# Batch 1's k and q loaded two pairs to a transfer, and w_out's copies made for two pieces at a time

## The chip, the cores and the metric

The kernel runs on one core of a Trainium2 chip. The metric is the time of one execution on the device in microseconds (us), the median of several runs. Beside them one execution was recorded by the hardware profiler; its rows are what is called the profile, or the trace, below. The engines are TensorE (PE for its matmuls, PEld for its weight loads), VectorE (DVE), ScalarE (ACT), GpSimd (POOL) and SyncE (SP), which here does nothing but issue transfers (DMAs). Sixteen DMA engines carry the transfers of the core.

## What is computed

An attention block with a threshold, and a feed-forward block behind it. All arrays are float32 except the two weights, which arrive as float64: their product with a float64 scalar makes them so.

```python
# q, k, v: (8 batches, 8 heads, 576, 64); tau = 0.02
scores = scale * np.matmul(q, k.transpose(0, 1, 3, 2))       # scale = 1/8
thresh = np.max(scores, axis=-1, keepdims=True) - tau
scores = np.where(scores >= thresh, scores, -1000000000.0)
scores = scores - np.max(scores, axis=-1, keepdims=True)
attn = np.exp(scores)
attn = attn / (np.sum(attn, axis=-1, keepdims=True) + 1e-09)
x = np.matmul(attn, v)                                       # -> (4608, 512), heads side by side
h = x @ w_in                                                 # w_in 512 x 1024
e = np.exp(h - np.max(h, axis=-1, keepdims=True))
solu = h * (e / (np.sum(e, axis=-1, keepdims=True) + 1e-09))
ln = (solu - mean(solu)) / np.sqrt(var(solu) + 1e-06) * g_ln
out = ln @ w_out                                             # w_out 1024 x 512
```

## The kernel before

**Tiling.** A head's 576 rows of 64 numbers are read as 64 rows of 576 (NK = 9 tokens to a row), and two heads, a pair, lie in the 128 partitions: head 0 in rows 0 to 63, head 1 in rows 64 to 127 (ROWS). There are 4 pairs in a batch (NP) and 32 in all. Scores need k and q turned, so that the 64 numbers of a head lie in the partitions (kT, qT).

**Rounds.** The program is one long loop over 144 rounds (rnd), 18 to a batch (PER). A round issues, in an order that is written out by hand and that each engine follows: the scores of one slot (line 399) after the turns that are due in front of them; the row maxima on VectorE (line 420); the threshold and the exponentials on ScalarE (lines 435 and 444); the sums and the normalising of the slot before on GpSimd (lines 451 to 454); a step of the feed-forward block, which is a half of x @ w_in (ff_h, line 570) or a half of ln @ w_out (ff_o, line 675); and the product of the weights with v (line 507) for a unit of two slots, LAG_PV = 3 rounds after its second slot (4 at slot 11). Then blocks turns the weights of the slot before on VectorE (line 466) and, every second round, sends them to their rows (wT, lines 475, 477 and 482). ff_swap moves rows of the feed-forward block in the same way (V, line 652).

**k and q.** Pairs of batch 0 are loaded whole in front of the loop (load_pair, line 133). Pairs of batch 1 are loaded by load_four, four heads at a time: for e = 0 and 1 a tile raw of 128 partitions receives head e of pair i in rows 0 to 63 and head e of pair i + 1 in rows 64 to 127 (j = 0 and 1, lines 141 and 142). The call stands in rounds 10 (k of pairs 4 and 5), 11 (q), 15 (k of pairs 6 and 7) and 16 (q). The turns that read them are matmuls with the identity (turn_beside, line 344), from round 14 and round 19 on; each needs both tiles of its k or q. Pairs of later batches come by load_natural (line 168) and are turned on VectorE and by copies (line 188).

**The weights.** w_in and w_out come in 16 pieces (piece): 0 to 7 are w_in's, 8 to 15 are w_out's. VectorE, ScalarE and GpSimd make float32 out of each (weight_e, weight_m, weight_b, weight_c). Of w_out there are two versions in the tile w2, of 16 entries: entry 2c is piece c as it is, and entry 2c + 1 is the same with the two halves of the partitions exchanged. weight_d makes the second with two transfers of 64 rows (line 312; both sides show up as `w` in the trace). It is called in the round after the piece is ready, so for c = 0 to 7 in rounds 8 to 15. ff_o reads entry m ^ r; its first half reads entries 0 to 7, its second half 8 to 15. It does not start before w2_done, which is set in round 15.

**Order on the queue.** All of these transfers are issued by SyncE, in program order. Within a round the order is: wT's copies, V's, the loads of raw weights, weight_d, and then what load_at holds for the round (load_four, load_v, load_natural). Each transfer can wait for what its source or its place is waiting for, and all behind it wait too. The completion of a transfer is told by one of eight semaphores, used in turn.

Of the kernel before, what the change touches and what calls it, by code (L numbers as in the profile page):

```python
# [20 lines left out]
def kernel(  # L21
# [27 lines left out]
    nc = tc.nc  # L49
# [10 lines left out]
    ROWS = (slice(0, 64), slice(64, P))  # L60
# [10 lines left out]
    w2 = const.tile([P, 2 * NC, DM], F32, name="w2")  # L71
# [63 lines left out]
    def load_four(i, nm):  # L135
        heads_of = rows_of[nm][P * i : P * i + 2 * P].rearrange("(j e p) n -> e j p n", j=2, e=2)
        for e in range(2):
            tag = "ends" if nm == "q" and i > NP else nm
            raw = loads.tile([P, NK * D], F32, tag=tag, bufs=BUFS[tag], name=nm)
            whole_rows[i, nm, e] = raw.rearrange("p (m d) -> p m d", m=NK)  # L140
            for j in range(2):
                nc.sync.dma_start(out=raw[ROWS[j]], in_=heads_of[e, j])

    def load_v(b, hf, parts):
        d = halves.setdefault((b, hf), {})
# [161 lines left out]

    def weight_d(x):
        c = x - 2 * NP
        if c >= 0:  # L310
            for r in range(2):
                nc.sync.dma_start(out=w2[ROWS[r], 2 * c + 1], in_=w2[ROWS[1 - r], 2 * c])

# [423 lines left out]
    for i, at, nm in ((NP, 10, "k"), (NP, 11, "q"), (NP + 2, 15, "k"), (NP + 2, 16, "q")):  # L739
        load_at.setdefault(at, []).append(lambda i=i, nm=nm: load_four(i, nm))  # L740
# [33 lines left out]
    with tc.manual_schedule():  # L774
# [45 lines left out]
        while True:  # L820
# [157 lines left out]
            if rnd - 1 in pieces:  # L978
                weight_d(pieces[rnd - 1])
                w2_done = pieces[rnd - 1] == NW - 1  # L980
# [36 lines left out]
```

## Time and profile before

| | |
|---|---|
| median of 3 runs | 858.18 us (855.24 to 861.62) |
| the profiled execution: its time, its span | 855.96 us, 854.2 us |
| mean granted TensorE clock | 0.987 |
| TensorE matmuls busy | 819.7 us, 96% of the span |
| VectorE, ScalarE, GpSimd busy | 680.4 us (80%), 572.3 us (67%), 499.1 us (58%) |
| DMA packets, bytes moved | 75442, 168.54 MB, mean 197 GB/s |
| line 142, k: 8 transfers of 144 KB | issued from 69.0 to 98.4 us, median 3.4 us to landing |
| line 142, q: 8 transfers of 144 KB | issued from 74.3 to 105.0 us, median 4.4 us to landing |
| line 312: 16 transfers of 128 KB | issued from 56.9 to 95.8 us, median 4.6 us to landing |

Busy is the time in which an engine had an instruction at work; matmuls are pipelined, so a busy TensorE need not be at its peak. The chain that ended last is followed back from the last instruction: at each step to what released it, or to the instruction before it on its engine. Landing is counted from the issue on the queue. A window is a stretch of the span, in us from its start.

### The profile page before, as it was taken

Reading aid. Unit: us, or ns where it says so; the run is one execution under the profiler, and the core shown is the slowest. Engines: PE = TensorE matmul, PEld = TensorE weight load, DVE = VectorE, ACT = ScalarE, POOL = GpSimd, SP = SyncE. Lnnn points to the kernel's source line nnn. Section 1 sums busy time; section 2 is a strip of 40 time slices with the busy share of each in tenths; the row PEclk is TensorE's granted clock in tenths of the full one; section 3 lists DMA queues with packets and bytes.
Section 4 is the critical chain, followed back from the end, with each engine's and each line's share of the span. In section 5 each row is a group of like instructions: output and inputs, shape, how many; then the busy total and the mean of one; then the engine's idle time right before and its main releaser. Section 6 shows DMA issues by size and latency. Waiting matters only on the chain.

```text
span 854.2 us, 36120 instructions
## 1 busy us (share of the span) xinstructions
PE 819.7 (96%) x15363; PEld 613.4 (72%) x15363; DVE 680.4 (80%) x1241; ACT 572.3 (67%) x1127; POOL 499.1 (58%) x945
## 2 busy tenths in 40 slices
PE   6679889999999999999999999999999999999997
PEld 5456666667677787777688877777777777777655
DVE  6999868889788888888788878888888888787361
ACT  6888857877666666666676667766667777775121
POOL 3888637666556656565566666565666655555120
PEclk8889999999999999999999999999999999999999
DMA  9989897898889788887889787888888887655212
GB/s 339 265 236 231 208 206 185 227 250 208 225 208 227 194 191 205 219 214 181 216 212 220 194 177 200 212 212 212 200 207 228 202 195 188 154 136 140 67 39 63
DMA packets 75442, 168.54 MB, mean 197 GB/s; under 512 B 11274, under 2 KB 32786, under 8 KB 75282
## 3 DMA queue, kind: packets, MB, share of 16 engines
q1 hardware_dynamic: 74994, 165.82, 77.3%
q8 instruction: 120, 1.97, 1.0%
q10 hardware_dynamic: 288, 0.43, 0.2%
q14 instruction: 40, 0.33, 0.1%
HBM read 46.14 MB, written 9.44 MB: 65 GB/s over the span
## 4 chain that ended last, share of the span: by engine, by line
PE 80%; DVE 7%; DMA 6%; ACT 3%; issue 2%; POOL 1%; SPq 1%; DVEq 0%; ACTq 0%
PE o_ps L675 27%; PE h_ps L570 21%; PE s_ps L399 15%; PE pv L507 14%; DMA wT<-T 4%; PE h_ps L560 3%; DVE T L466 2%; DVE w L420 2%; ACT w L435 1%; ACT w L444 1%; DVE w L290 1%; DMA V<-u 1%; POOL w L454 0%; PE tp L336 0%; SPq L482 0%
## 5 line engine op out<-in xcount | busy, mean ns | idle before, releaser
L435 ACT ACTIVATE w<-s_ps,nth 128x576 f32<-128x576 f32 x280 | 196.9, 738 | 110.5 <-DVE nth L420 92.0
L675 PE MATMUL o_ps<-w,uT 64*64 64x256 f32 x4608 | 268.4, 376 | 1.3 <-DVE uT L662 0.6
L675 PEld LDWEIGHTS o_ps<-w,uT 64*64 64x64 f32 x4608 | 221.0, 133 | 55.2 <-ACT xh L537 12.0
L420 DVE CUSTOM_DVE_ANT_0 w<-s_ps,tau_t 128x576 f32<-128x576 f32 x280 | 200.1, 751 | 73.7 <-PE s_ps L399 46.3
L454 POOL TENSOR_SCALAR w<-w,sm 128x576 f32<-128x576 f32 x288 | 221.3, 780 | 14.3
L466 DVE STREAM_TRANSPOSE T<-w 128x576 f32<-128x576 f32 x288 | 207.7, 756 | 24.4 <-POOL w L454 23.7
L570 PE MATMUL h_ps<-w,xh 64*64 64x512 f32 x1856 | 220.4, 590 | 0.0
L444 ACT ACTIVATE w<-w,ntau 128x576 f32<-128x576 f32 x288 | 219.5, 766 | 0.0
L507 PEld LDWEIGHTS pv<-wT,v 64*64 64x64 f32 x5760 | 170.4, 135 | 40.7 <-issue 22.9
L399 PE MATMUL s_ps<-kT,qT 64*64 64x64 f32 (+1 forms) x2048 | 173.5, 415 | 16.6 <-ACT w L435 12.5
L507 PE MATMUL pv<-wT,v 64*64 64x128 f32 (+1 forms) x5760 | 173.1, 263 | 7.2 <-DMA wT<-T 5.0
L570 PEld LDWEIGHTS h_ps<-w,xh 64*64 64x64 f32 x1856 | 114.5, 133 | 81.4 <-issue 52.1
L451 POOL TENSOR_SCALAR sm<-sm 128x2 f32<-128x2 f32 x144 | 36.2, 252 | 194.5 <-ACT w L444 191.1
L452 POOL TENSOR_TENSOR sm<-sm,mone 128x2 f32<-128x2 f32 x144 | 108.2, 751 | 12.0
L399 PEld LDWEIGHTS s_ps<-kT,qT 64*64 64x64 f32 x2048 | 70.5, 137 | 25.4 <-ACT w L435 18.0
L537 ACT COPY xh<-pv 128x256 f32<-128x256 f32 x64 | 25.4, 397 | 72.5 <-PE pv L507 72.4
L636 ACT ACTIVATE V<-u,nb,rs 128x1024 f32<-128x1024 f32 x36 | 44.7, 1241 | 41.3 <-POOL nb L626 34.8
L662 DVE STREAM_TRANSPOSE uT<-V 128x1024 f32<-128x1024 f32 x36 | 44.3, 1231 | 21.4 <-DMA V<-u 20.7
L444 ACT ACTIVATION_READ_ACCUMULATOR w<-w,ntau 128x1 f32 x288 | 55.3, 192 | 0.0
L600 DVE TENSOR_TENSOR u<-h_ps,u 128x1024 f32<-128x1024 f32 x36 | 42.8, 1189 | 9.9 <-ACT u L594 9.9
L641 DVE TENSOR_SCALAR u<-u,rs,nb 128x1024 f32<-128x1024 f32 x36 | 34.9, 969 | 17.5 <-ACT V L636 17.4
L594 ACT ACTIVATE u<-h_ps,hm 128x1024 f32<-128x1024 f32 x36 | 40.2, 1117 | 9.9 <-DMA V<-u 5.6
(81 smaller groups left out, 563.7 us busy)
## 6 DMA issues: line engine op xcount, KB each, us to landing
wT<-T SPq DMA_DIRECT2D x160, 288.0 KB, 6.7
wT<-T SPq DMA_DIRECT2D x64, 576.0 KB, 5.5
v<-in_v_dram SPq DMA_DIRECT2D x16, 576.0 KB, 5.7
V<-u SPq DMA_DIRECT2D x144, 64.0 KB, 3.4
out_dram<-ob SPq DMA_DIRECT2D x71, 128.0 KB, 2.6
q<-in_q_dram SPq DMA_DIRECT2D x28, 288.0 KB, 6.0
k<-in_k_dram SPq DMA_DIRECT2D x27, 288.0 KB, 6.5
qT<-flip SPq DMA_DIRECT2D x48, 144.0 KB, 3.5
```

Source lines behind the costliest of these rows:

```text
L399: nc.tensor.matmul(out=ps[h][ROWS[y], ks], lhsT=lhsT, rhs=d["kT"][ROWS[h], ks], start=True, stop=True,)
L420: nc.vector.tensor_tensor_reduce(out=w, in0=ps[:, 0:S], in1=(zero if loose else tau_t).to_broadcast([P, S]), scale=1.0, scalar=BIG, op0=AL ...
L435: nc.scalar.activation(out=d["w"][x], in_=d["w"][x] if d["loose"] else d["ps"][x][:, 0:S], func=AF.Prelu, bias=d["nth"][x], scale=-1.0, al ...
L444: nc.scalar.activation(out=w, in_=w, func=AF.Exp, bias=ntau, scale=1.0, accum_out=sm[:, x : x + 1])
L452: nc.gpsimd.tensor_tensor(out=sm, in0=sm, in1=mone, op=ALU.pow)
L454: nc.gpsimd.tensor_scalar(out=w, in0=w, scalar1=sm[:, x : x + 1], scalar2=1.0, op0=ALU.mult, op1=ALU.mult)
L466: nc.vector.transpose(out=T[:, :, r, h, :], in_=w)
L507: nc.tensor.matmul(out=to, lhsT=d["v"][ROWS[u], (h0 + h - u) % 4, m,], rhs=rhs, start=m == 0, stop=m == NK - 1,)
L570: mm = nc.tensor.matmul(out=h[ROWS[y], f], lhsT=x[ROWS[r], c, ROWS[y]], rhs=w1_parts[ROWS[r], c, part ^ r], start=part == 0 and c == 0, st ...
L636: nc.scalar.activation(out=V, in_=u, func=AF.Identity, bias=nb, scale=rs)
L662: nc.vector.transpose(out=uT, in_=d["V"].rearrange("p y (m x) -> p m y x", x=32))
L675: nc.tensor.matmul(out=d["o"][ROWS[z], 512 * (r ^ other) : 512 * (r ^ other) + 256], lhsT=d["uT"][ROWS[r], m].rearrange("p y x -> p (y x)" ...
```

## The change

load_four makes one transfer out of the two of a tile: the destination is all 128 partitions of raw, and the source is heads_of[e], whose dimensions are j (2 blocks, 128 rows of the array apart), p (64 rows that follow each other) and n (576 numbers). load_four is called four times, so 16 transfers of 144 KB become 8 of 288 KB.

weight_d does nothing for an even c (and for pieces of w_in, as before). For an odd c it copies pieces c - 1 and c together, once for each half of the partitions: 64 rows, two entries, 512 numbers. So 16 transfers of 128 KB become 8 of 256 KB, and the copies for c = 0, 2, 4 and 6 are made one round later than before.

```diff
@@ load_four @@
             whole_rows[i, nm, e] = raw.rearrange("p (m d) -> p m d", m=NK)
-            for j in range(2):
-                nc.sync.dma_start(out=raw[ROWS[j]], in_=heads_of[e, j])
+            nc.sync.dma_start(out=raw, in_=heads_of[e])
@@ weight_d @@
         c = x - 2 * NP
-        if c >= 0:
+        if c > 0 and c % 2:
+            pair_of = w2.rearrange("p (c two) n -> p two c n", two=2)[:, :, c - 1 : c + 1]
             for r in range(2):
-                nc.sync.dma_start(out=w2[ROWS[r], 2 * c + 1], in_=w2[ROWS[1 - r], 2 * c])
+                nc.sync.dma_start(out=pair_of[ROWS[r], 1], in_=pair_of[ROWS[1 - r], 0])
```

## The prediction

> **What bounds the kernel now.** I read the page first, then the stretches of rounds 10 to 20, then that stretch of each queue. One core, no second die to compare.
>
> ```profile
> span 854.2 us, 36120 instructions
> PE 819.7 (96%) x15363; PEld 613.4 (72%) x15363; DVE 680.4 (80%) x1241; ACT 572.3 (67%) x1127; POOL 499.1 (58%) x945
> ...
> q1 hardware_dynamic: 74994, 165.82, 77.3%
> ```
>
> TensorE is busy 96% of the span, and the chain that ended last is 80% TensorE. So a stall of TensorE is not made good later; a saving elsewhere is worth only what TensorE waits for. The edited lines run between about 57 and 106 us, so I read the table by stretches there (columns: stretch, its length, busy us of each engine with counts, granted clock, DMA share, GB/s):
>
> ```profile
> 0.00:20.00 20.00, 13.00 (x210) 9.53 (x212) 11.70 (x28) 12.09 (x23) 7.06 (x21) 0.91 0.92 340
> 20.00:45.00 25.00, 17.96 (x309) 12.65 (x309) 24.18 (x52) 21.36 (x42) 20.92 (x26) 0.77 1.02 277
> 69.00:85.00 16.00, 15.76 (x270) 11.14 (x262) 15.96 (x33) 13.93 (x28) 14.05 (x21) 1.00 0.96 235
> 97.00:111.00 14.00, 13.09 (x305) 11.38 (x304) 12.08 (x25) 9.37 (x19) 9.63 (x19) 1.00 0.89 236
> ```
>
> From 69 to 85 us TensorE and VectorE are both full and the DMA engines are 96% taken: no engine has room there, nor have the transfers. The chain of waits in order of time says what ends last (start, length, what):
>
> ```profile
> 86.69 0.61 SPq L477
> 87.29 0.04 issue
> 87.34 6.85 DMA wT<-T
> 94.19 0.04 issue
> 94.23 2.03 PE pv L507 x65
> ...
> 108.19 9.76 DMA wT<-T
> 117.96 4.37 DMA V<-u
> ```
>
> The copies wT (lines 475 to 482) and V (line 652) take 4 to 10 us to land because transfers are queued ahead of them, and twice in these rounds the chain goes through them. They have no slack worth the name. All of them leave from SyncE's queue, the one that carries the edited transfers; its timeline shows the order:
>
> ```profile
> 66.97 1.99 SPq L312 DMA_DIRECT2D w<-w  x2
> 69.01 2.52 SPq L142 DMA_DIRECT2D k<-in_k_dram  x4
> 71.64 1.02 SPq L248 DMA_DIRECT2D raw<-in_moe_w_out_dram  x1
> 73.18 1.12 SPq L312 DMA_DIRECT2D w<-w  x2
> 74.35 2.52 SPq L142 DMA_DIRECT2D q<-in_q_dram  x4
> 76.97 0.60 SPq L475 DMA_DIRECT2D wT<-T  x1
> ...
> 96.48 2.52 SPq L142 DMA_DIRECT2D k<-in_k_dram  x4
> 102.24 3.40 SPq L142 DMA_DIRECT2D q<-in_q_dram  x4
> ```
>
> And TensorE's timeline shows when they are needed: the first turn of k (line 344) at 78.6, of q at 85.0, the first product on the wT copy issued at 76.97 at 86.8 us:
>
> ```profile
> 78.61 1.45 PE L344 MATMUL s_ps<-ident,k 64*64 64x64 f32 x50
> 86.83 2.66 PE L507 MATMUL pv<-wT,v 64*64 64x128 f32 x72
> 105.88 1.48 PE L344 MATMUL s_ps<-ident,k 64*64 64x64 f32 x50
> ```
>
> **The copies of w_out (weight_d).** Sixteen transfers become eight of twice the size: the same bytes in the same 2048 B rows, 64 rows ahead as before. The copies of pieces 0, 2, 4 and 6 move one round later. That costs nothing as long as line 675 is later still. Its first half reads pieces 0 to 3 and starts at 97.97; the second, from 102.42, reads pieces 4 to 7, whose last copies are issued at 95.25 and take 4.7 us by the median of such copies here: 2.5 us of cover. SyncE saves little, for the issue of a transfer grows with its rows (0.6 us for 64 rows of k, 1.06 for the 128 of line 168). One thing moves: two copies (1.99 us at 66.97) no longer stand ahead of k in round 10, so k is issued near 67.0. Sum: zero, with a gain of at most 2 us.
>
> **The loads (load_four).** Four transfers of 64 rows become two of 128 rows; rows and bytes are the same. What changes is the shape of the source: its leading dimension was 64 (rows that follow each other) and becomes 2 (two blocks of 64 rows, 128 rows apart). Every transfer over 4 KB on the page has at least 32 rows in front. The trace has no row for a leading dimension of 2, so I bound it by two ends. At the near end the transfer is spread over all 16 engines like lines 133 and 142. At the far end its rows are dealt out by the leading dimension, and two engines carry it. The view of the DMA issues is a hint, no proof: it gives a landing time for all groups but these two, the only ones with fewer than 32 rows (1 and 8):
>
> ```profile
> tau_row<-in_tau_dram SPq DMA_DIRECT2D x1, 0.0 KB
> g_rows<-in_moe_g_ln_dram SPq DMA_DIRECT2D x1, 4.0 KB
> ```
>
> So transfers with few rows in front complete differently, and a leading dimension of 2 is nearer to these two rows than to 64. I take two engines. [...]
>
> Cost of a packet: in the first 20 us, nearly all loads from DRAM, 340 GB/s at a share of 0.92 over 16 engines is 23.1 GB/s for a busy engine, 0.100 us for the 2304 B of one row. From 69 to 85 us it is 235/(16 x 0.96) = 15.3 GB/s, 0.151 us. I take 0.100, since two engines with the rest waiting meet little contention, and keep 0.151 for the range. A transfer then holds two engines for 64 x 0.100 = 6.4 us, the two of one load_four for 12.8, where 16 engines spent 1.6. From issue to landing a 64-row load takes at least 2.8 us, 0.4 of it packets; I put 1.2 of the rest behind the last packet.
>
> *First pair of loads.* On the two engines the wT copies issued at 63.3 to 66.9 are done at about 69.5. Then k runs to 82.3 and lands at 83.5; needed at 78.6: TensorE 4.9 late. Behind it raw (8 packets an engine, 1.4 us) and two w copies (1.4): 85.1. q: 12.8 more, lands at 99.1, needed at 85.0: 14.1 late. The wT copies issued from 76.97 (16 packets of 4608 B, 3.2 to 4.8 us, take 4) land at 103.1, needed at 86.8: **16.3 late**. These are lags against one timetable, so the largest counts, not their sum. Then the backlog is gone.
>
> *Second pair* (rounds 15 and 16). Everything there is needed 16.3 later, but SyncE's queue is late too: it issues in order, and a transfer waits for one issued eight before it (the queue's waits below: a wT copy waits for a weight load that it does not read).
>
> ```profile
> SPq L652 <- DMA wT<-T: 1.8, 2, 1.0
> SPq L477 <- DMA raw<-in_moe_w_out_dram: 1.1, 1, 1.1
> ```
>
> So the third wT copy of round 14 waits for q (99.1), V and the w copies follow, and k goes out near 108.5 instead of 96.5. It lands at 108.5 + 1.2 + 12.8 + 1.2 = 123.7 against 105.9 + 16.3 = 122.2: 1.5 late. The next wT copies: 127.7 against 124.5, 3.2 late. q behind them: 126.5 + 12.8 + 1.2 = 140.5 against 110.9 + 16.3 = 127.2: **13.3 late**. The later wT copies (146.1 against 137.1) and V (148.6 against 138.6) follow, less late.
>
> *Clock.* The granted clock was 0.77 from 20 to 45 us, where TensorE was busy 72%, and 1.00 from 69 us. With stalls of some 30 us in the next 70, matmuls between them could run at less: 15 us of them at 0.77 would be 4.5 more. I take 2. [...]
>
> **Sum.** 16.3 + 13.3 + 2 = 31.6 us. On the profiled execution (855.96, its span 854.2 and 1.8 around it) this gives 887.6; that run lies 2.2 under the median of three (855.24 to 861.62), so I name 858.2 + 31.6 = **890 us**.
>
> **The rivals.** *Sixteen engines, a queue relieved.* If the source's leading dimension does not matter, k and q land as now, and SyncE saves two thirds of a microsecond here and there. Place: the wT copies in rounds 12 to 18. TensorE waits 3.3 us for them from 60 to 130 us; saving part of it gives 856, all of it and the 5.5 us that VectorE waits for V, 849. It decides if a new transfer lands within 7 us. For it: bytes and row sizes are unchanged. Against it: the two rows without a landing time. This is the case that is not slower. *Two engines, another pair for each transfer.* Then the two of a load_four run side by side, 6.4 instead of 12.8: k is in time, q lands at 86.3 (1.3 late), wT at 90.3 (3.5 late), and the second pair's q 4.8 late: 8 in all, 866 us. Nothing in the trace shows which engines a transfer takes. *Two engines and dear packets,* 0.151 us: k to 88.8, raw and copies to 93.0, q to 112.3, wT lands at 118.3, 31.5 late; the second pair by the same steps some 26; 916 us. For it: the share of 0.96 at these rounds; against it: the others wait while two engines work.
>
> **How the numbers follow.** Forecast 0.68; sixteen engines 0.12; other pairs 0.08; dear packets 0.12. A change of 1% (8.6 us) is about what a measurement of this kernel can tell. Slower by over 1%: forecast, dear packets and half of the other pairs, 0.84. Within 1%: the other half and most of the sixteen, 0.13. Faster: 0.03. The range runs from 862 (part of the other pairs) to 914 (up to the dear packets) and leaves out the sixteen and the tail of the dear packets, under 0.2.
>
> **What would show it.** Right: the new k and q land over 7 us after issue, TensorE waits at line 344 for k and q and at line 507 for wT, some 16 us around 80 to 105 and some 13 around 120 to 145, and the DMA share of those stretches falls far below 0.9 while it is the only thing moving. The rest of the span has the same length as before. Wrong: line 141 lands in about 6 us like line 133, or TensorE's work ends on time although they land late.

## The result, and the profile after

The changed kernel takes **895.8 us** (median of 6 runs, 894.5 to 898.96) against 859.0 for the kernel before in the same comparison: a ratio of 1.0428, interval 1.0388 to 1.0468, or 36.8 us. The prediction was 890 us, within 862 to 914.

The page of the changed kernel, and two of the stretches that were shown of before (stretch, its length, busy us of each engine with counts, granted clock, DMA share, GB/s):

```profile
span 894.5 us, 36097 instructions
PE 832.2 (93%) x15363; PEld 635.9 (71%) x15363; DVE 679.4 (76%) x1241; ACT 573.2 (64%) x1127; POOL 498.9 (56%) x945
...
q1 hardware_dynamic: 74626, 165.82, 74.0%
```

```profile
69.00:85.00 16.00, 10.80 (x166) 5.49 (x156) 11.65 (x22) 10.32 (x21) 12.74 (x21) 0.99 0.43 112
97.00:111.00 14.00, 6.41 (x142) 5.66 (x142) 2.72 (x6) 1.97 (x6) 2.55 (x3) 0.63 0.56 129
```

Bytes are the same as before. From 69 to 85 us TensorE works 10.80 us instead of 15.76, and the DMA share is 0.43 instead of 0.96: everything waits, the transfers too. A narrower stretch, asked of the same kernel, shows what is still moving:

```profile
80.00:85.00 5.00, 0.00 (x0) 0.00 (x0) 0.65 (x1) 1.00 (x4) 3.22 (x6) 0.98 0.13 47
```

A share of 0.13 of 16 engines is as much as two engines at work throughout; no view names the engines. If it is two, they move 47 GB/s, 23.5 each, which is 0.098 us for a row of 2304 B, and TensorE does nothing.

TensorE's waits from 60 to 190 us (who waited for what: us in all, times, longest), and its timeline at the turns (line 344; the wait ahead of a group stands in brackets):

```profile
PE s_ps L344 <- DMA q<-in_q_dram: 20.0, 4, 8.9
PE s_ps L344 <- DMA k<-in_k_dram: 12.4, 2, 6.6
PE pv L507 <- DMA wT<-T: 0.8, 2, 0.6
```

```profile
85.65 2.56 PE L344 MATMUL s_ps<-ident,k 64*64 64x64 f32 x48 [5.85 <-DMA k<-in_k_dram]
95.38 0.33 PE L344 MATMUL s_ps<-ident,q 64*64 64x64 f32 x2 [0.62 <-DMA q<-in_q_dram]
104.59 1.71 PE L344 MATMUL s_ps<-ident,q 64*64 64x64 f32 x32 [8.88 <-DMA q<-in_q_dram]
107.97 2.67 PE L507 MATMUL pv<-wT,v 64*64 64x128 f32 x72
...
132.82 2.56 PE L344 MATMUL s_ps<-ident,k 64*64 64x64 f32 x48 [6.55 <-DMA k<-in_k_dram]
142.87 0.47 PE L344 MATMUL s_ps<-ident,q 64*64 64x64 f32 x2 [2.11 <-DMA q<-in_q_dram]
151.75 1.71 PE L344 MATMUL s_ps<-ident,q 64*64 64x64 f32 x32 [8.41 <-DMA q<-in_q_dram]
```

The turns wait 32.4 us for k and q, which they did not do at all before. The queue of SyncE (start, length of the issues) and the chain of waits name the same two loads:

```profile
67.43 1.63 SPq L141 DMA_DIRECT2D k<-in_k_dram  x2
...
75.38 9.12 SPq L141 DMA_DIRECT2D q<-in_q_dram  x2
84.62 5.22 SPq L475 DMA_DIRECT2D wT<-T  x1
89.88 2.62 SPq L477 DMA_DIRECT2D wT<-T  x2
```

```profile
76.12 28.42 DMA q<-in_q_dram
...
124.67 27.03 DMA q<-in_q_dram
```

The second transfer of q lands 28.4 us after its issue in the first place and 27.0 in the second; the groups of line 142 took 3.4 and 4.4 by their medians. And the issue itself holds the queue: two issues of q take 9.12 us, where four took 2.52. Behind the two places the rest is as it was: from 200 to 854 us the changed kernel has TensorE busy for 649.0 us, the kernel before from 160 to 814 us for 649.7.

### The profile page after: what moved, and what is told of

Same layout as the page of the kernel before. It is cut to its first block, busy times and chain, and to the rows that moved or that the text cites. A ratio compares the mean times of both kernels' runs of the same rounds, so it can differ in the third digit from the quotient of the medians.

```text
span 894.5 us, 36097 instructions
## 1 busy us (share of the span) xinstructions
PE 832.2 (93%) x15363; PEld 635.9 (71%) x15363; DVE 679.4 (76%) x1241; ACT 573.2 (64%) x1127; POOL 498.9 (56%) x945
## 4 chain that ended last, share of the span: by engine, by line
PE 79%; DMA 10%; ACT 2%; SPq 2%; DVE 2%; POOL 2%; issue 1%; DVEq 0%; ACTq 0%
PE o_ps L675 25%; PE h_ps L570 21%; PE s_ps L399 15%; PE pv L507 14%; DMA q<-in_q_dram 6%; DMA wT<-T 3%; PE h_ps L560 3%; ACT w L435 1%; ACT w L444 1%; DVE T L466 1%; POOL w L454 1%; SPq L475 1%; DVE w L420 1%; PE s_ps L344 1%; SPq L477 1%
## 5 line engine op out<-in xcount | busy, mean ns | idle before, releaser
L675 PEld LDWEIGHTS o_ps<-w,uT 64*64 64x64 f32 x4608 | 226.2, 133 | 51.7 <-ACT xh L537 11.9
L466 DVE STREAM_TRANSPOSE T<-w 128x576 f32<-128x576 f32 x288 | 207.5, 755 | 23.2 <-POOL w L454 20.5
L507 PEld LDWEIGHTS pv<-wT,v 64*64 64x64 f32 x5760 | 175.0, 136 | 35.2 <-issue 18.9
L399 PE MATMUL s_ps<-kT,qT 64*64 64x64 f32 (+1 forms) x2048 | 181.8, 426 | 14.9 <-ACT w L435 12.3
L507 PE MATMUL pv<-wT,v 64*64 64x128 f32 (+1 forms) x5760 | 175.9, 264 | 3.6 <-DMA wT<-T 3.3
L570 PEld LDWEIGHTS h_ps<-w,xh 64*64 64x64 f32 x1856 | 120.0, 134 | 80.4 <-issue 48.0
L451 POOL TENSOR_SCALAR sm<-sm 128x2 f32<-128x2 f32 x144 | 36.8, 256 | 210.1 <-ACT w L444 206.8
L399 PEld LDWEIGHTS s_ps<-kT,qT 64*64 64x64 f32 x2048 | 75.6, 140 | 19.8 <-ACT w L435 16.2
```

The lines of the kernel that those rows point to most:

```text
L399: nc.tensor.matmul(out=ps[h][ROWS[y], ks], lhsT=lhsT, rhs=d["kT"][ROWS[h], ks], start=True, stop=True,)
L466: nc.vector.transpose(out=T[:, :, r, h, :], in_=w)
L507: nc.tensor.matmul(out=to, lhsT=d["v"][ROWS[u], (h0 + h - u) % 4, m,], rhs=rhs, start=m == 0, stop=m == NK - 1,)
L570: mm = nc.tensor.matmul(out=h[ROWS[y], f], lhsT=x[ROWS[r], c, ROWS[y]], rhs=w1_parts[ROWS[r], c, part ^ r], start=part == 0 and c == 0, st ...
L675: nc.tensor.matmul(out=d["o"][ROWS[z], 512 * (r ^ other) : 512 * (r ^ other) + 256], lhsT=d["uT"][ROWS[r], m].rearrange("p y x -> p (y x)" ...
```

## The experiments

**The two halves of the change, each alone.** First the loads, with weight_d as before:

```diff
-        if c > 0 and c % 2:
-            pair_of = w2.rearrange(...)[:, :, c - 1 : c + 1]
+        if c >= 0:
             for r in range(2):
-                nc.sync.dma_start(out=pair_of[ROWS[r], 1], in_=pair_of[ROWS[1 - r], 0])
+                nc.sync.dma_start(out=w2[ROWS[r], 2 * c + 1], in_=w2[ROWS[1 - r], 2 * c])
```

> Only the loads of k and q are changed; the copies of w_out are made as before. Theory (two engines carry a load whose source has two blocks in front): nearly the whole loss is here, 1.035 to 1.048 of before, some 33 to 38 us, with line 141 waited for by TensorE for over 30 us. Rival (the copies, made a round later and twice as large, hold up the queue): at least a third of the loss goes, under 1.03.

Measured: 894.5 us, 1.0434 of before (1.0387 to 1.0481). Then the copies, with the loads as before:

```diff
-            nc.sync.dma_start(out=raw, in_=heads_of[e])
+            for j in range(2):
+                nc.sync.dma_start(out=raw[ROWS[j]], in_=heads_of[e, j])
```

> Only the copies of w_out are changed; k and q are loaded in four transfers as before. Theory (two engines for the loads): no part of the loss, 0.997 to 1.003 of before. Rival (the copies hold up the queue): slower by 10 us or more, 1.012 and up.

Measured: 858.1 us, 1.0013 (0.9981 to 1.0045). The loads are the whole loss. The copies cost nothing and bring nothing that can be measured, though SyncE issues half as many of them.

**The number of blocks in front.** Three runs keep the number of transfers, their rows, bytes, order and place, and alter only into how many evenly spaced blocks the 128 rows of a source are cut. Which row of a head lands where changes with it, so these kernels do not compute the attention that is asked for.

```diff
-        heads_of = rows_of[nm][...].rearrange("(j e p) n -> e j p n", j=2, e=2)
+        heads_of = rows_of[nm][...].rearrange("(x e p) n -> e x p n", x=4, e=2)    # and 8, and 16
```

> As the changed kernel, but the source of a load is four blocks of 32 rows instead of two of 64: the same number of transfers, rows, bytes and row sizes, on the same queue at the same place. The rows of batch 1's heads are thereby put in another order, so its values are others. Theory (the engines are as many as the blocks in front): four engines, 32 packets of 0.1 us each, 3.2 us a transfer and 6.4 for two; k in time, q 1 to 3 us late, the wT copies behind it 2 to 4 us late: 1.004 to 1.014 of before. Rival (a load of 128 rows in blocks is slow as such, or SyncE is held up by its size): as slow as the changed kernel, 1.04.

> As the changed kernel, but the source of a load is eight blocks of 16 rows; the rows of batch 1's heads are thereby in another order, so its values are others. Theory (as many engines as blocks in front): 16 packets an engine, 1.6 us a transfer and 3.2 for two, 6 us or more under the four-block run's lateness of some 4 us in each place: k and q in time, 0.998 to 1.006 of before. Rival (something other than the number of engines grows with the size of a block): between the sixteen and the four, near 1.01.

> As the changed kernel, but the source of a load is sixteen blocks of 8 rows: again the same transfers, rows and bytes, with the rows of batch 1's heads in another order, so its values are others. Theory (as many engines as blocks in front): sixteen engines, as before: 0.995 to 1.004 of before, and a time to landing under 7 us. Rival (a load in blocks is slow as such): 1.02 to 1.045. Rival (an even worse spread, since each block is smaller): 1.045 and up.

Sixteen blocks: 0.9998 (0.9964 to 1.0032), and the loads land in 6.9 us by the median, as the transfers of 288 KB did in the kernel before (q 6.0, k 6.5, wT 6.7 us by the medians):

```profile
L141 SPq DMA_DIRECT2D q<-in_q_dram x4: 645/997/1870, 72.6 to 103.3; - x4
...
DMA to landing us min/median/max: 4.4/6.9/10.7
```

Four blocks: 1.0192 (1.0135 to 1.0249). Eight: 1.0088 (1.0054 to 1.0122). Both miss what the theory expected of them on the high side, and both have the order that it demands. Two rivals (a load in blocks or of 128 rows is slow as such) are out: sixteen blocks cost nothing. But with eight the time is the one that the last rival named, near 1.01: by the times alone, something else that grows with the size of a block would do as well. The DMA share decides between them. While only the rest of such a backlog moves, the share stays on one value, which was 0.13 in the changed kernel (0.13 to 0.14 in each us from 80 to 86). First a stretch of the run with four blocks, then two short ones, of 1 us each, of the run with eight:

```profile
86.00:90.00 4.00, 2.25 (x36) 1.27 (x27) 3.97 (x9) 3.53 (x8) 3.65 (x8) 1.00 0.27 102
```

```profile
88.00:89.00 1.00, 0.65 (x24) 0.65 (x26) 0.88 (x2) 0.13 (x2) 0.84 (x2) 0.96 0.54 171
113.00:114.00 1.00, 1.00 (x34) 0.85 (x34) 0.00 (x0) 0.37 (x1) 0.70 (x4) 1.00 0.53 171
```

Of 16 engines these shares are 2.1, 4.3 and 8.5 to 8.6: as many as there are blocks in front. In the run with eight, TensorE waits more for the wT copies behind the loads than for q (for wT, it waited 4.1 us in the kernel before and 5.2 with sixteen blocks):

```profile
PE pv L507 <- DMA wT<-T: 7.2, 6, 2.4
PE s_ps L344 <- DMA q<-in_q_dram: 2.4, 2, 1.2
```

One sum comes near all four. At the 0.100 us of the prediction, eight transfers of 128 rows on n engines hold each of these for an estimated 8 x 128/n x 0.100 us; sixteen engines would be held for 6.4. Extra time of the busiest engines, and what was lost (ratio less one, times 857 us):

| blocks | engine time, us | extra, us | lost, us |
|---|---|---|---|
| 2 | 51.2 | 44.8 | 36.7 |
| 4 | 25.6 | 19.2 | 16.5 |
| 8 | 12.8 | 6.4 | 7.5 |
| 16 | 6.4 | 0 | -0.2 |

With four, eight and sixteen blocks the loss is this extra time within its interval; with two it is 8 us less. Nearly all that the busiest engines have to do in addition is lost. I had taken off the time by which the loads are issued ahead of their use. By this sum that lead is worth little in these rounds.

**One kind of load at a time.**

```diff
-            nc.sync.dma_start(out=raw, in_=heads_of[e])
+            if nm == "k":                     # and nm == "q" in the other run
+                nc.sync.dma_start(out=raw, in_=heads_of[e])
+                continue
+            for j in range(2):
+                nc.sync.dma_start(out=raw[ROWS[j]], in_=heads_of[e, j])
```

> Of the loads only k's are made in one transfer, q's in four pieces as before. Theory (a backlog on two engines, of which the lead of 8 to 10 us covers a part once): k 5 to 6.5 us late in each place and nothing later than that, with a little of the clock: 1.012 to 1.018 of before, and this run and that with q alone together lose less than the changed kernel. Rival (every two-engine load costs its own 10 us): 1.021, half of the loss.

> Of the loads only q's are made in one transfer, k's in four pieces as before. Theory (a backlog on two engines): q 4 to 6 us late and the wT copies behind it 6 to 9 in each place, with a little of the clock: 1.014 to 1.022 of before; together with k alone 22 to 34 us, less than the 36.8 of the changed kernel. Rival (every two-engine load costs its own 10 us): 1.021, and the two together as much as the changed kernel.

k alone: 872.5 us, 1.0187 (1.0164 to 1.0209). q alone: 876.5 us, 1.0239 (1.0210 to 1.0268). The two parts lose 16.0 and 20.5 us, 36.5 together, as much as the changed kernel. A backlog of which the lead covers a part once would have made the parts lose less than the whole, so this speaks for the rival. It does not settle the matter alone: each part lies above the theory's range by less than its interval, and the rival's 1.021 for each is not met exactly either. By the sum above, the k loads have 22.4 us of extra engine time and so have those of q; they cost it less some 6 and 2 us.

**The same loads three rounds earlier.**

```diff
-    for i, at, nm in ((NP, 10, "k"), (NP, 11, "q"), (NP + 2, 15, "k"), (NP + 2, 16, "q")):
+    for i, at, nm in ((NP, 7, "k"), (NP, 8, "q"), (NP + 2, 12, "k"), (NP + 2, 13, "q")):
```

> The changed kernel with its four load_four calls three rounds earlier (rounds 7, 8, 12 and 13), so that k and q have some 15 us more. Theory (two engines are blocked for everything behind on the queue): TensorE no longer waits for k and q, but the wT copies, raw weights and V behind them on the same queue are late by 8 to 15 us in each of the two places: 1.015 to 1.035 of before. Rival (only k and q themselves come late): the loss is gone, 0.997 to 1.006.

Measured: 895.3 us, 1.0448 (1.0422 to 1.0474), as slow as the changed kernel and above the 1.015 to 1.035 that the theory gave. TensorE no longer waits for k or q at all; it waits for the wT copies instead (waits from 40 to 190 us, and the two longest in the timeline):

```profile
PE pv L507 <- DMA wT<-T: 36.6, 7, 14.9
```

```profile
73.11 4.39 PE L507 MATMUL pv<-wT,v 64*64 64x128 f32 x70 [10.85 <-DMA wT<-T]
133.64 4.37 PE L507 MATMUL pv<-wT,v 64*64 64x128 f32 x70 [14.88 <-DMA wT<-T]
```

So the cause is not that k and q come late. Two engines and the queue are held (an issue of q took up to 6.5 us here too), and whoever is next on them pays. The theory is right on who waits and wrong on how much: the loss is 38.4 us of the 44.8, not a part that the lead would leave. This run does not part the held engines from the held queue. The run with four blocks does: there no issue of these loads took over 1.13 us, and 16.5 us were lost, so busy engines are enough.

**The clock.** In the changed kernel the mean granted clock falls to 0.63 in the stretches with waits, and matmuls take longer (48 turns of k 2.56 us, where 50 took 1.45). Two runs fill the waits with idle matmuls to hold the clock up. In both, the slots of rounds 14 and 20 compute the scores of the slot after them, since the added loop reuses the variable r; the amount of work is the same.

```diff
         kept = {}
         x = S
+        for y in range({14: 12, 15: 20, 19: 14, 20: 22}.get(s, 0)):     # second run: 7, 11, 8, 13
+            for r in range(2):
+                for z in range(2):
+                    nc.tensor.matmul(
+                        out=ps[r][ROWS[z], 0:SM], lhsT=ident[ROWS[r], ROWS[z]],   # second run: S:1024
+                        rhs=w1[ROWS[r], 0, 0:SM],             # second run: 0 : 1024 - S
+                        start=True, stop=True,
+                    )
```

> The changed kernel with idle matmuls (48, 80, 56 and 88 of 64x512, 5.1 to 9.4 us at full clock) in front of the turns of rounds 14, 15, 19 and 20, where TensorE waits for k and q; their sums are overwritten by the scores. They fit into the waits that the changed kernel showed (5.9, 9.5, 6.6 and 10.5 us). Theory (some 10 us of the loss are matmuls at a lower granted clock, because TensorE stands still): the clock of those stretches rises from 0.63 to over 0.9 and the time falls by 6 to 10 us, to 1.031 to 1.037 of before. Rival (the lower clock costs nothing, since the transfers decide anyhow): 1.041 to 1.05.

Measured: 1.0652 (1.0623 to 1.0681). This run says nothing on the clock: the idle matmuls took 10.5 to 19.4 us each time, twice my estimate of 5.1 to 9.4 (the 48 in front of the first wait stand in the trace as 96), and overran the waits. The second run has the right amount.

> As the run with idle matmuls, but with as many as fit: each of the program's float32 matmuls stands in the trace as two, so the run before had twice the time meant (10.5, 17.5, 12.2 and 19.4 us) and overran the waits. Here 28, 44, 32 and 52 of 64x448, some 5.3, 8.4, 6.1 and 9.9 us at full clock, into the free columns that the turns overwrite, in the changed kernel's waits of 5.9, 9.5, 6.6 and 10.5 us. Theory (about 10 us of the loss are matmuls at a lower granted clock): clock of those stretches over 0.9 and 1.031 to 1.038 of before. Rival (the lower clock costs nothing on the path): 1.041 to 1.05.

Measured: 895.1 us, 1.0456 (1.0426 to 1.0486). The clock was up while the waits were filled (first the changed kernel, then this run, in the stretch from 126 us; from 85 to 97 us it was 1.00 instead of 0.72). From 97 to 111 us, with the rest of a wait and the work behind it, it was only 0.76 instead of 0.63:

```profile
126.00:140.00 14.00, 7.45 (x140) 6.66 (x140) 3.13 (x9) 2.74 (x6) 3.67 (x8) 0.63 0.27 83
```

```profile
126.00:140.00 14.00, 13.87 (x244) 9.34 (x240) 4.26 (x9) 5.03 (x10) 3.58 (x9) 1.00 0.32 95
103.68 1.71 PE L344 MATMUL s_ps<-ident,q 64*64 64x64 f32 x32 [3.81 <-DMA q<-in_q_dram]
150.41 1.71 PE L344 MATMUL s_ps<-ident,q 64*64 64x64 f32 x32 [4.13 <-DMA q<-in_q_dram]
```

Nothing is gained. The turns of q begin at 103.68 and 150.41 us, where they began at 104.59 and 151.75: when q lands is settled by the transfers, and what TensorE does before, slowly or quickly, only fills the wait. My theory of some 10 us for the clock falls. The clock behind the last wait of each place was low in this run too (a wait of 4 us was left, and 32 turns of q took the same 1.71 us), so that part was not taken away. It can be read off the changed kernel instead: from the turn of q to the next work it takes 3.4 us (104.59 to 107.97, 151.75 to 155.13) at a granted clock of 0.50, before 1.85, so some 1.5 us in each place. That this is all of the clock's cost was not tested by a run of its own. At the first wait for k the granted clock was 0.98 from 80 to 85 us, in the wait, and 0.50 from 87 to 89, behind it.

## Why the prediction was right

**Two engines.** Right, and the choice on which everything hung: between transfers of 32 rows and more in front, and those of 1 and 8, it went to the lower end. The evidence for it was thinner than it looked (see the last section). That rows are dealt out by the blocks in front was my estimate, and no view names the engines of a transfer; what the runs show is the DMA share, 0.13 with two blocks, 0.27 with four, 0.53 to 0.54 with eight. The chance of 0.12 for sixteen engines went to a case that did not occur, nor did other pairs of engines for each transfer: then two transfers would have run side by side, and the share from 80 to 85 us would have been 0.25.

**A packet at 0.100 us.** Right while two engines work alone (0.098). In the second transfer of q it was more: it landed 9.2 us after the first, where 6.4 was forecast. From 92 to 104 us the share was 0.87, since the wT copies and others had been issued meanwhile. Over 64 packets 9.2 us is 0.144 us each, nearly the 0.151 that I had kept for the upper end of the range; that contention made the difference is not shown by a run.

**First pair of loads.** Forecast 16.3, came 19.2 (TensorE's lag at the next turn of k, 125.97 against 105.88, less the 0.9 that it had before the first). k was forecast 4.9 late, waited 5.9. q was forecast to land at 99.1 and came at 104.6: this is the term that was too small, by some 2 us for k ahead of it (85.6 instead of 83.5) and 2.8 for its own second transfer. The wT copies were forecast to decide with 4 us behind q, and here the path was wrong: the product on them began without a wait, 3.4 us after the turn of q, and from 60 to 190 us TensorE waited 0.8 us for wT. Whether they or q decide seems to make little difference to what is lost: with the earlier loads it was wT, and the loss was the same.

**Second pair of loads.** Forecast 13.3, came 20.2 (40.3 at the end of the span, less the 20.1 by then). Here a step failed: I let SyncE's queue be late by 12 us only, against a timetable 16.3 late, and so gave the second pair of loads a lead of 4.3 us. The first k load of round 15 was issued at 115.70, not at 108.5; before it was 96.48, so it came 19.2 late, against a timetable 20.1 late. The wait that I had named did come: the third wT copy of round 14 stood for the landing of q, until 104.56 where I had 99.1. What I had left out comes behind it: V, whose source VectorE had not written, stood until 110.57. The queue's waits from 60 to 200 us and its timeline, then VectorE's:

```profile
SPq L477 <- DMA q<-in_q_dram: 7.4, 1, 7.4
...
SPq L652 <- DVE u L641: 4.8, 2, 4.6
```

```profile
104.56 0.55 SPq L477 DMA_DIRECT2D wT<-T  x1
110.57 3.62 SPq L652 DMA_DIRECT2D V<-u  x4
114.29 1.36 SPq L312 DMA_DIRECT2D w<-w  x2
115.70 1.94 SPq L141 DMA_DIRECT2D k<-in_k_dram  x2
```

```profile
108.23 0.76 DVE L420 CUSTOM_DVE_ANT_0 w<-s_ps,tau_t 128x576 f32<-128x576 f32 x1 [12.71 <-PE s_ps L399]
```

VectorE waits for TensorE's scores, these for q, so the queue comes late by nearly as much as TensorE does.

**The clock.** Forecast 2, came some 3 by the reading above, though I had matmuls between the stalls in mind, and it is those behind the last wait that cost.

**The copies.** Forecast zero with a gain of at most 2; came 1.0013, no gain. That an issue grows with its rows holds for the two times named in the prediction and not in general: for 128 rows line 133 took SyncE 0.33 to 0.71 us in the kernel before, line 168 0.33 to 2.41.

The sum was 31.6. The medians differ by 36.8; the two profiled executions, on which the readings above were made, differ by 40.3, for that of before lay below its median (855.96 us, median 859.0). The forecast was short by the two terms named, the landing of q in the first pair and the lead of the second. In both I treated the loads as late against a timetable with some lead in it; from 69 to 85 us TensorE, VectorE and the transfers were all full, as my own first table showed, and nothing there could absorb a delay. The simpler sum, the extra engine time of 44.8 us with nothing taken off, would have been 8.0 too high where mine was 5.2 too low.

## What to carry to other kernels

Before joining transfers, look at the outermost dimension of the source, not at the bytes: joining two blocks with a gap between them put a 2 there, and loads of 288 KB went at 47 GB/s and a DMA share of 0.13, two engines' worth. With 2, 4, 8 and 16 blocks in front 36.7, 16.5, 7.5 and -0.2 us were lost. The destination had 128 rows in front in every run, so its part was not tried. Where the DMA engines are nearly full, as here (0.96), cost such a load by the time of its busiest engine and take little off for issuing it early: three rounds earlier the loss was 38.4 us, and TensorE waited 36.6 us for the wT copies behind. The lower clock between waits was a symptom here, where transfers set the timetable: with 1.00 instead of 0.63 from 126 to 140 us the time was 1.0456 of before, against 1.0428.

## What was not expected of the hardware

**The queue itself is held.** With the joined loads of the changed kernel outstanding, the issue of a further transfer took SyncE up to 8.4 us (line 141, q) instead of some 0.6, and the issue of the next wT copy 5.2. Meanwhile the share fell to the 0.13 above, so most of the sixteen engines were idle. With four, eight and sixteen blocks the longest issue of these loads was 1.1, 1.7 and 1.9 us. How many transfers fit before the issue is held was not tried.

**The landing times are a weak sign.** The joined loads have none in any kernel with two, four or eight blocks, and have one with sixteen. That fits the hint in the prediction, two rows of 1 and 8 rows without one. But on the pages of the changed kernel and of the runs with four and eight blocks no transfer has one, the copies of 64 rows included, while with the loads alone changed the others have theirs (wT 6.3 us). A missing landing time alone does not tell a transfer with few engines; the share of 0.13 does better.
